# First queries and keys loaded behind the last weights, and one way of making the power of two for all 16 pieces

## The chip, the cores and the metric

The kernel runs on one core of a Trainium2 chip. The core has a matrix engine (PE, TensorE), a vector engine (DVE), a scalar engine (ACT), a general engine (POOL, GpSimd) and a queue engine (SP) that here issues all the transfers. The engines run their own instruction streams in order and wait for one another through semaphores. The metric is the device time of one execution in microseconds; the reported number is the median of several executions.

## The reference

Top-k attention feeds a two-layer perceptron. Cut to what matters, the functions put in a row:

```python
batch, n_heads, seq, head_dim = (8, 8, 576, 64)
top_k = 32
scores = scale * np.matmul(q, k.transpose(0, 1, 3, 2))
kth = np.partition(scores, -top_k, axis=-1)[..., -top_k:-top_k + 1]
mask = scores >= kth
scores = np.where(mask, scores, -1000000000.0)
scores = scores - np.max(scores, axis=-1, keepdims=True)
attn = np.exp(scores)
attn = attn / (np.sum(attn, axis=-1, keepdims=True) + 1e-09)
attn_out = np.matmul(attn, v).astype(np.float32)
...
x = np.ascontiguousarray(attn_out.transpose(0, 2, 1, 3)).reshape(B * S, H * D)
h = x @ w_in
g = np.maximum(0.01 * h, h)
return (g @ w_out).astype(np.float32)
```

x has 4608 rows of 512 numbers, w_in is 512 x 2048 and w_out 2048 x 512.

q, k and v are float32. The two weight matrices come out of `randn(...) * (1.0 / np.sqrt(...))` and are float64, so the kernel has to round 16 MB of 64-bit numbers to float32 before it can use them.

## The kernel before

**The opening: 16 pieces of weights.** The weights lie in DRAM as 16 pieces of 128 x 1024 float64 numbers, 1024 KB each (pieces 0 to 7 are w_in, 8 to 15 are w_out). A double is read as four 16-bit words. `load_weights` (L107 issues the transfer) brings a piece into one of three buffers called raw. `round_weights` is a generator with three parts, and the loop over n at the end of the kernel runs part one of piece n, part two of piece n-1 and part three of piece n-2 in each turn:

- part one: POOL copies the highest word of each number into a tile called top (L124, two buffers); ACT turns the middle words into the destination tile (L125) and the low words into a bf16 tile (L127).
- part two: DVE takes the exponent out of top into the tile scale (L129). For pieces 0 to 13 ACT then makes the power of two from it with the exponential function (L132). For pieces 14 and 15 two DVE instructions make it instead, a clamp and a shift of the exponent into a bf16's place (L135, L136). DVE also takes the mantissa bits (L137) and the sign (L138) out of top; PE adds the three parts of the mantissa in PSUM with six matmuls against scaled identities (L148 to L150).
- part three: DVE joins sign and power of two (L152) and multiplies the sum in PSUM by it into the destination tile (L155; two instructions for pieces 13 and 15, whose sums lie in two tiles).

A transfer into a raw buffer waits until POOL and ACT have read the piece three before. POOL's copy of piece n waits until DVE's L152 of piece n-2 has read the top tile it overwrites.

**Queries and keys.** The 64 heads are taken as 32 pairs. `load_qk(pi)` issues two transfers of 288 KB on SP (L168 for q, L169 for k). In the kernel before, the pairs 0 to 3 are loaded in the turns n = 6 to 9 of the weight loop, each directly behind `load_weights(n + 3)`, so that they stand on SP's queue between the pieces 9 and 13. Everything on SP's queue is issued in the order in which it is written.

**The first scores.** `first_scores(u)` computes the scores of one block of 128 queries: eight short matmuls on PE (L236), then two copies from PSUM on ACT (L241). It is called for the first block in turn n = 13 and for the second in turn n = 16. In the order of ACT's stream, the copies of the first block stand between the exponential of piece 12 and the first activation of piece 14; on PE, its matmuls stand between the sums of piece 12 and those of piece 13.

**The main part.** 144 units follow, one step each. In a step DVE finds the 32 largest scores per row (`top_k`: L250, L255, L258), POOL masks the rest (L268, L269), ACT exponentiates (L272) and normalizes (L284), the result is transposed by DMA through DRAM (L293, L294, L298) or on PE in haste (L308, L314), PE weighs the values (L335), and chunks of finished tokens go through the perceptron on PE (L391 for the first layer, L403 for the second; L359 and L375 for the first two chunks). The order of all this is written out by hand; PE gets portions of perceptron work in fixed slots of each step.

Of the kernel before, what the change touches and what calls it, by code (L numbers as in the profile page):

```python
# [12 lines left out]
BF16 = mybir.dt.bfloat16  # L13
AF = mybir.ActivationFunctionType
ALU = mybir.AluOpType
# [5 lines left out]
def kernel(  # L21
# [13 lines left out]
    nc = tc.nc  # L35
# [9 lines left out]
    HP = DMODEL // P  # L45
# [30 lines left out]
    LN2 = math.log(2.0)  # L76
    least = const.tile([P, 1], F32, name="least")
# [8 lines left out]
    NPIECE = 2 * HP * DFF // WCH  # L86
# [3 lines left out]
    def piece(n):  # L90

        if n < NPIECE // 2:
            j, c = divmod(n, HP)
            return w_in[c][:, j * WCH:(j + 1) * WCH]
        f = 2 * (n - NPIECE // 2)
        return w_out[f // 4][:, f % 4:f % 4 + 2, :].rearrange("p g n -> p (g n)")
# [12 lines left out]
    def round_weights(n):  # L109

        raw = raw_of.pop(n)
        dst = piece(n)
        mid = raw[:, :, 2]
        low = raw.rearrange("p n w -> p (n w)").bitcast(U32).rearrange("p (n w) -> p n w", w=2)[:, :, 0]
        top = raws.tile([P, WCH], U16, name="top", bufs=2)
        scale = raws.tile([P, WCH], U16, name="scale", bufs=2)  # L120
        parts = work.tile([P, 2 * NKC - 1, P], F32, name="wT", bufs=3)
        parts = parts.rearrange("p c n -> p (c n)").bitcast(U16)
        m_top, m_low = parts[:, 0:WCH], parts[:, WCH:2 * WCH].bitcast(BF16)
        nc.gpsimd.tensor_copy(top, raw[:, :, 3])  # L124
        nc.scalar.activation(dst, mid, AF.Copy, bias=-7.0 - 2.0 ** -16, scale=2.0 ** -20)  # L125

        nc.scalar.activation(m_low, low, AF.Copy, bias=128.0, scale=2.0 ** -29)  # L127
        yield
        nc.vector.tensor_scalar(scale, top, 4, 0x7FF, ALU.logical_shift_right, ALU.bitwise_and)  # L129
        if n < NPIECE - 2:  # L130

            nc.scalar.activation(scale.bitcast(BF16), scale, AF.Exp, bias=least, scale=LN2)  # L132
        else:

            nc.vector.tensor_scalar(scale, scale, 1151.0, 896.0, ALU.min, ALU.max)  # L135
            nc.vector.tensor_scalar(scale, scale, 896.0, 128.0, ALU.subtract, ALU.mult)  # L136
        nc.vector.tensor_scalar(m_top, top, 0xF, 0x3F80, ALU.bitwise_and, ALU.bitwise_or)  # L137
        nc.vector.tensor_scalar(top, top, 0x8000, None, ALU.bitwise_and)  # L138
        if n < NPIECE - 4 or n % 2 == 0:
            tag, bufs = ("wide", 2) if n < NPIECE - 4 else ("narrow", 1)  # L140
            pw = ps_sc.tile([P, 2, 512], F32, name=tag, bufs=bufs)
            sums = [(pw[:, h, :], h * 512) for h in range(2)]
            ends = [(pw.rearrange("p h n -> p (h n)"), 0)]
        else:
            ends = sums = [(ps_ml.tile([P, 512], F32, name="pw", tag="ml"), h * 512) for h in range(2)]
        for pw, c in sums:
            at = slice(c, c + 512)
            nc.tensor.matmul(pw, ident_top, m_top[:, at].bitcast(BF16), start=True, stop=False)  # L148
            nc.tensor.matmul(pw, ident, dst[:, at], start=False, stop=False)
            nc.tensor.matmul(pw, ident_low, m_low[:, at], start=False, stop=True)  # L150
        yield
        nc.vector.tensor_tensor(scale, scale, top, ALU.bitwise_or)  # L152
        for pw, c in ends:
            at = slice(c, c + pw.shape[-1])
            nc.vector.tensor_tensor(dst[:, at], pw, scale[:, at].bitcast(BF16), ALU.mult)  # L155
# [5 lines left out]
    def load_qk(pi):  # L161
        if pi % (LOADED + 3) < LOADED:
            qt = loads.tile([P, S], F32, name="qt")
            kt = loads.tile([P, S], F32, name="kt")
        else:
            raw = raws.tile([P, WCH, 4], U16, name="raw").rearrange("p n w -> p (n w)").bitcast(F32)
            qt, kt = raw[:, 0:S], raw[:, S:2 * S]
        nc.sync.dma_start(qt, qT[pi])  # L168
        nc.sync.dma_start(kt, kT[pi])  # L169
        qk_of[pi] = qt, kt  # L170
# [314 lines left out]
    with tc.manual_schedule():  # L485
        last = {p: n for n, u in enumerate(steps) for p in u.pairs}

        def load_more(s):

            for of, load, n, lag in ((v_of, load_v, LOADED_V, LAG + 1), (qk_of, load_qk, LOADED + 3, 8)):  # L490
                while len(of) < NPAIR and (len(of) < n or last[len(of) - n] + lag <= s):
                    load(len(of))
                    if lag > LAG + 1 and len(of) > n:
                        break


        for n in range(3):
            load_weights(n)
        rounding = {}
        for n in range(NPIECE + 2):  # L500
            for i in (n, n - 1, n - 2) if AS_WORDS else ():
                if 0 <= i < NPIECE:
                    if i == n:
                        rounding[i] = round_weights(i)
                    next(rounding[i], None)
            load_weights(n + 3)
            if 6 <= n < 6 + HP:
                load_qk(n - 6)
            elif n == NPIECE - 3:
                first_scores(steps[0])  # L510
            elif n == NPIECE:
                first_scores(steps[1])
            if n == NPIECE - 1:
                load_v(0)
                load_v(1)

        def weights_of(u):
            reciprocals(u)
            normalize(u, 0)
            normalize(u, 1)  # L520

        def values(*place):
            due = [u for n, u in enumerate(steps) if values_at(n) == place]
            if due:
                po = ps_sc.tile([P, 2, 512], F32, name="wide", bufs=2)[:, 0, 0:2 * P]
                po = po.rearrange("p (u n) -> p u n", u=2)
            else:
                return ()
            for n, u in enumerate(due):
                weigh_values(u, po[:, n, :])  # L530
            return [(u, po[:, n, :]) for n, u in enumerate(due)]

        def keep(weighed, *place):
            for u, po in weighed:
                keep_values(u, po)
            attended(*place)

        for s in range(len(steps) + LAG + 1):
            cur, old, older, new = unit(s), unit(s - 1), unit(s - 2), ()
            if s % 2 == 0:  # L540
                new = [u for u in steps[s + 2:s + 4] if u]
            picks = top_k(cur) if cur else iter(())
            budget = slot_budget(s)

            def slot():
                next(picks, None)

            at_first = s < HURRY and s - 2 in HURRIED
            if at_first:
                weights_of(older)  # L550
            slot()
            if old:
                mask(old, 0)
                mask(old, 1)
            late = s < HURRY and not {s - 1, s - 2} & set(HURRIED)
            if older and not late and not at_first:
                weights_of(older)
            mlp_steps(budget)
            weighed = values(s, MIDDLE)
            at_once = s - 2 in HURRIED or any(at == (s, MIDDLE) for at, _ in ready_at)  # L560
            if at_once:
                keep(weighed, s, MIDDLE)
            slot()
            if older and late:
                weights_of(older)
            if s - 2 in HASTY:
                transpose_in_haste(older)
            mlp_steps(budget)
            if old:
                exponents(old, 0)  # L570
            mlp_steps(budget)
            if older:
                keep_transposed(older) if s - 2 in HASTY else transpose(older, lambda: mlp_steps(budget))
            if not older or s - 2 in HASTY:
                mlp_steps(budget)
            slot()
            slot()
            mlp_steps(budget)
            if old:
                exponents(old, 1)  # L580
                sums(old)
            mlp_steps(budget)
            if not at_once:
                keep(weighed, s, MIDDLE)
            if new and s < HURRY:
                scores(new)
            keep(values(s, END), s, END)
            if new and s >= HURRY:
                scores(new)
            budget = slot_budget(s + 1)  # L590
            mlp_steps(budget)
            load_more(s)
        mlp_steps(1e9)
# [58 lines left out]
```

## Time and profile before

| what | value | from |
|---|---|---|
| median of four executions | 1471.62 us | the times |
| lowest, highest | 1469.85, 1472.03 us | the times |
| the profiled execution's own time | 1469.85 us | the times |
| its span, first to last instruction | 1468.0 us | page, head |
| mean granted PE clock over the span | 0.980 | view of the cores |
| PE, DVE, ACT, POOL busy | 1394.6, 1321.5, 1098.1, 1096.2 us | page, part 1 |
| weight loop: from the first transfer's issue to the first `top_k` | 0.72 to 64.69 us | timelines of SP and DVE |
| DVE idle ahead of `rz` (L281), waiting for ACT | 45.0 us in 45 places, the longest 7.7 us | waits of DVE, from 64 us on |
| PE idle from 130 to 240 us | 4.5 us in five places | waits of PE |

What the engines do in stretches of the opening, in us of busy time:

| stretch | PE | DVE | ACT | POOL | GB/s moved |
|---|---|---|---|---|---|
| 10 to 20 | 9.99 | 7.76 | 10.00 | 2.77 | 338 |
| 20 to 30 | 8.44 | 9.27 | 10.00 | 3.63 | 337 |
| 30 to 40 | 8.09 | 8.87 | 9.30 | 3.21 | 407 |
| 40 to 50 | 8.50 | 9.27 | 7.90 | 3.62 | 414 |
| 50 to 60 | 7.30 | 8.70 | 8.56 | 2.63 | 392 |
| 60 to 70 | 8.21 | 9.76 | 3.54 | 0.24 | 110 |

A timeline row gives start and duration in us, the engine, the line, the operation, what it writes and reads, and in brackets the idle time ahead of it with what ended it. Instructions of one engine overlap a little, so a row's duration can be longer than the distance to the next start; sums are made from the starts.

### The profile page before, as it was taken

The numbers are of one execution on the slowest core, as the hardware profiler recorded it, in microseconds if no ns is written. First come the engines' busy times: TensorE is split into PE (matmuls) and PEld (weight loads), VectorE is DVE, ScalarE is ACT, GpSimd is POOL, SyncE is SP. The second block draws the span as 40 slices with busy tenths as digits, with TensorE's granted clock in tenths as the row PEclk, the third lists the DMA queues.
The fourth block names the chain that finished last, engine by engine and source line by source line (L and its number), as shares of the span: only waits on it lengthen the run. The fifth ranks groups of instructions, "written<-read, shape, count | busy, mean of one in ns | idle before, by whom it ended". The sixth has DMA issues, their size and how long they took to land.

```text
span 1468.0 us, 24094 instructions
## 1 busy us (share of the span) xinstructions
PE 1394.6 (95%) x8066; PEld 927.7 (63%) x8068; DVE 1321.5 (90%) x3400; ACT 1098.1 (75%) x1979; POOL 1096.2 (75%) x743
## 2 busy tenths in 40 slices
PE   7717999999999999999999999999999999999999
PEld 2304548575767676767676767666666666666674
DVE  6999999999999999999999999999999999999600
ACT  8657888777887777777777777777777777777710
POOL 3288888888788888787888887878787878787700
PEclk9957999999999999999999999999999999999999
DMA  9724443655366455664566555765457545664510
GB/s 345 287 75 134 138 120 100 187 148 141 96 194 189 137 137 155 171 185 137 146 166 185 151 137 124 195 179 150 126 161 208 137 138 138 162 140 134 148 45 14
DMA packets 388795, 222.29 MB, mean 151 GB/s; under 512 B 333888, under 2 KB 333888, under 8 KB 386624
## 3 DMA queue, kind: packets, MB, share of 16 engines
q1 hardware_dynamic: 388672, 220.77, 53.3%
q8 instruction: 63, 1.03, 0.3%
q14 instruction: 60, 0.49, 0.1%
HBM read 46.14 MB, written 92.01 MB: 94 GB/s over the span
## 4 chain that ended last, share of the span: by engine, by line
PE 80%; DVE 15%; DMA 2%; ACT 1%; issue 1%; POOL 0%; DVEq 0%; ACTq 0%; SPq 0%
PE ph L391 31%; PE pz L403 31%; PE wide L335 10%; DVE tops L255 6%; PE wide L220 6%; DVE pairs L258 5%; PE narrow L220 3%; DVE pairs L250 2%; DMA raw<-in_weights_dram 1%; DMA wT<-apart 1%; DVE w_in L155 1%; DVE scale L152 1%; DVE w_out L155 0%; DVE scale L129 0%; DVE top L138 0%
## 5 line engine op out<-in xcount | busy, mean ns | idle before, releaser
L268 POOL TENSOR_SCALAR pen<-s_sb,tops 128x576 f32<-128x576 f32 x288 | 637.5, 2213 | 208.2 <-DVE tops L255 140.1
L255 DVE MAX8 tops<-pairs 128x8 f32<-128x288 f32 (+1 forms) x1152 | 635.8, 591 | 0.0
L403 PE MATMUL pz<-w_out,gT 128*128 128x512 f32 x1152 | 504.7, 594 | 2.4 <-ACT scale L364 2.4
L391 PE MATMUL ph<-x,w_in 128*128 128x256 f32 x2176 | 482.9, 381 | 0.0
L258 DVE MATCH_REPLACE8 pairs<-tops,pairs 128x288 f32<-128x288 f32 (+1 forms) x864 | 460.0, 537 | 0.0
L391 PEld LDWEIGHTS ph<-x,w_in 128*128 128x128 f32 x2176 | 409.4, 190 | 76.7 <-issue 22.2
L269 POOL TENSOR_TENSOR s_sb<-s_sb,pen 128x576 f32<-128x576 f32 x288 | 406.5, 1411 | 24.1
L403 PEld LDWEIGHTS pz<-w_out,gT 128*128 128x128 f32 x1152 | 216.4, 190 | 267.2 <-issue 262.8
L293 ACT COPY split<-s_sb 128x1152 uint16<-128x1152 uint16 x280 | 309.4, 1146 | 0.0
L284 ACT ACTIVATE s_sb<-s_sb,rz 128x576 f32<-128x576 f32 x288 | 207.6, 773 | 46.8 <-DVE rz L281 46.8
L272 ACT ACTIVATE s_sb<-s_sb,nbias 128x576 f32<-128x576 f32 x288 | 222.3, 772 | 13.8 <-POOL s_sb L269 13.8
L250 DVE TENSOR_TENSOR pairs<-s_sb 128x576 f32<-128x576 f32 x288 | 213.3, 779 | 9.9
L335 PEld LDWEIGHTS wide<-wT,vt 128*64 128x64 f32 x3200 | 161.7, 139 | 66.8 <-issue 34.5
L335 PE MATMUL wide<-wT,vt 128*64 128x128 f32 (+1 forms) x3200 | 179.4, 268 | 24.0 <-ACT s_sb L227 21.1
L227 ACT COPY s_sb<-wide 128x704 f32<-128x704 f32 x142 | 107.1, 755 | 21.1 <-PE wide L220 21.0
L397 ACT ACTIVATE gT<-ph 128x512 f32<-128x512 f32 x136 | 80.6, 592 | 54.2 <-PE ph L391 53.5
L349 ACT COPY x<-wide 128x128 f32<-128x128 f32 (+1 forms) x160 | 32.2, 260 | 111.6 <-PE wide L335 111.4
L220 PE MATMUL wide<-kt,qt 64*128 64x352 f32 (+1 forms) x392 | 75.8, 496 | 26.4 <-ACT s_sb L227 23.6
L412 ACT COPY o_sb<-pz 128x512 f32<-128x512 f32 x36 | 21.0, 585 | 97.3 <-PE pz L403 95.1
L227 ACT COPY s_sb<-narrow 128x448 f32<-128x448 f32 x142 | 68.7, 536 | 0.7
L281 DVE RECIPROCAL rz<-ze 128x2 f32<-128x2 f32 x144 | 22.2, 154 | 45.1 <-ACT ze L277 45.0
L258 DVE MATCH_VALUE_LOAD pairs<-tops,pairs 128x8 f32 x864 | 62.5, 72 | 0.0
(63 smaller groups left out, 621.6 us busy)
## 6 DMA issues: line engine op xcount, KB each, us to landing
apart<-split SPq DMA_DIRECT2D x280, 288.0 KB, 2.1
raw<-in_weights_dram SPq DMA_DIRECT2D x16, 1024.0 KB, 6.7
vt<-in_vk_dram SPq DMA_DIRECT2D x32, 320.0 KB, 3.4
out_dram<-o_sb SPq DMA_DIRECT2D x36, 256.0 KB, 2.6
qt<-in_qT_dram SPq DMA_DIRECT2D x20, 288.0 KB, 3.2
kt<-in_kT_dram SPq DMA_DIRECT2D x20, 288.0 KB, 3.7
raw<-in_qT_dram SPq DMA_DIRECT2D x12, 288.0 KB, 3.6
raw<-in_kT_dram SPq DMA_DIRECT2D x12, 288.0 KB, 3.7
```

Of the source, the lines that this page charges most:

```text
L220: nc.tensor.matmul(to[r0:r0 + u.rows, i, :], qt[d, u.q0:u.q0 + u.rows], kt[d, k0:k1], start=True, stop=True)
L250: nc.vector.tensor_tensor(pairs[:, :, n, :], u.both[:, :, 0:HS], u.both[:, :, HS:S], op)
L255: nc.vector.max(out=u.tops[:, i, r, :], in_=rest[i])
L258: nc.vector.match_replace(out=rest[i], in_to_replace=u.tops[:, i, r, :], in_values=rest[i], imm_value=LOWEST)
L268: nc.gpsimd.tensor_scalar(pen, u.s[i], u.tops[:, i, ROUNDS - 1, 7:8], MASKED, ALU.is_lt, ALU.mult)
L269: nc.gpsimd.tensor_tensor(u.s[i], u.s[i], pen, ALU.add)
L272: nc.scalar.activation(u.s[i], u.s[i], AF.Exp, bias=u.nbias[:, i:i + 1], scale=SCALE, accum_out=u.z[:, i:i + 1])
L284: nc.scalar.activation(u.s[i], u.s[i], AF.Copy, bias=0.0, scale=u.rz[:, i:i + 1])
L293: nc.scalar.copy(split, pairs[:, :, h])
L335: nc.tensor.matmul(po[side * D:(side + 1) * D, o, :], vt[:, c, side, :], u.wT[:, c + side * NKC if c + 1 < NKC else c, r:r + n], start=(c ...
L391: nc.tensor.matmul(ph[:, i, 0:n], w_in[c][:, f * P:(f + 1) * P], x[c][:, 0:n], start=(c == 0), stop=(c == HP - 1),)
L403: nc.tensor.matmul(pz[0:m, 0:DMODEL], gT[:, f, r0:r0 + m], w_out[f // 4][:, f % 4, :], start=(f == 0), stop=(f == NFC - 1),)
```

## The change

All 16 pieces take the exponential on ACT; the two DVE instructions for pieces 14 and 15 are gone. The four pairs of q and k are issued in the turns n = 12 to 15, the first of them behind the last weight transfer. The first block's scores are computed one turn later, n = 14 instead of 13.

```diff
@@ round_weights
         nc.vector.tensor_scalar(scale, top, 4, 0x7FF, ALU.logical_shift_right, ALU.bitwise_and)
-        if n < NPIECE - 2:
-
-            nc.scalar.activation(scale.bitcast(BF16), scale, AF.Exp, bias=least, scale=LN2)
-        else:
-
-            nc.vector.tensor_scalar(scale, scale, 1151.0, 896.0, ALU.min, ALU.max)
-            nc.vector.tensor_scalar(scale, scale, 896.0, 128.0, ALU.subtract, ALU.mult)
+
+        nc.scalar.activation(scale.bitcast(BF16), scale, AF.Exp, bias=least, scale=LN2)
         nc.vector.tensor_scalar(m_top, top, 0xF, 0x3F80, ALU.bitwise_and, ALU.bitwise_or)
@@ the weight loop
             load_weights(n + 3)
-            if 6 <= n < 6 + HP:
-                load_qk(n - 6)
-            elif n == NPIECE - 3:
+
+            if NPIECE - HP <= n < NPIECE:
+                load_qk(n - NPIECE + HP)
+            if n == NPIECE - 2:
                 first_scores(steps[0])
             elif n == NPIECE:
                 first_scores(steps[1])
```

The order of instructions that comes of it: SP issues 16 weight transfers in a row, then the eight of q and k, then the values as before. PE does the first block's eight matmuls between the sums of pieces 13 and 14 (before: 12 and 13). ACT's stream at the end of the loop becomes

```
before: ... L132 of 12 | L241 x2 (first block) | L125, L127 of 14 | L132 of 13 | L125, L127 of 15 | L241 x2 (second block)
after:  ... L132 of 12 | L125, L127 of 14 | L132 of 13 | L241 x2 (first block) | L125, L127 of 15 | L132 of 14 | L132 of 15 | L241 x2 (second block)
```

(the lines named as in the kernel before). Behind that, every engine's instructions are the same and in the same order.

## The prediction

> **What bounds the kernel now.** I read the page's chain of waits first, then the chain in order of time where it changes engine, then the timelines of DVE, ACT and PE around the end of the weight loop.
>
> ```profile
> span 1468.0 us, 24094 instructions
> PE 80%; DVE 15%; DMA 2%; ACT 1%; issue 1%; POOL 0%; DVEq 0%; ACTq 0%; SPq 0%
> ```
>
> ```profile
> 208.53 0.85 DVE pairs L258 x2
> 209.38 0.08 DVE rz L281
> 209.47 0.02 issue
> 209.49 0.79 ACT s_sb L284
> 210.27 0.04 issue
> 210.32 0.66 PE wide L308 x4
> ```
>
> The chain is on DVE until 209.5 us and on PE from there to the end, where PE is busy 1252.0 of 1255 us. So a microsecond that DVE gains before 209 us starts PE's long stretch a microsecond sooner, and nothing behind it is touched by the change. PE itself starts that stretch behind DVE: its sums from 128 us on wait for ACT copies that DVE paces. From 64.69 to 209 us DVE is busy without a wait the profile charges to another engine. What matters is thus the start of the first `top_k` (L250), at 64.69 us.
>
> DVE's rows ahead of it, pieces 13 to 15 of the weights:
>
> ```profile
> 50.89 0.42 DVE L137 TENSOR_SCALAR wT<-top 128x1024 uint16<-128x1024 uint16 x1
> 51.34 0.43 DVE L138 TENSOR_SCALAR top<-top 128x1024 uint16<-128x1024 uint16 x1
> 52.34 0.69 DVE L152 TENSOR_TENSOR scale<-scale,top 128x1024 uint16<-128x1024 uint16 x1 [0.57 <-ACT scale L132]
> ...
> 58.71 0.43 DVE L129 TENSOR_SCALAR scale<-top 128x1024 uint16<-128x1024 uint16 x1
> 59.17 0.43 DVE L135 TENSOR_SCALAR scale<-scale 128x1024 uint16<-128x1024 uint16 x1
> 59.63 0.43 DVE L136 TENSOR_SCALAR scale<-scale 128x1024 uint16<-128x1024 uint16 x1
> 59.97 0.42 DVE L137 TENSOR_SCALAR wT<-top 128x1024 uint16<-128x1024 uint16 x1
> ...
> 64.69 1.42 DVE L250 TENSOR_TENSOR pairs<-s_sb 128x576 f32<-128x576 f32 x2
> ```
>
> One wait, 0.57 us for an exponential, and otherwise DVE runs straight through: it sets the pace, 3.26 us a piece (47.29 to 50.55 from one L129 to the next). ACT's and PE's rows in the same stretch:
>
> ```profile
> 49.06 1.18 ACT L125 ACTIVATE w_out<-raw 128x1024 f32<-128x1024 uint16 x1 [0.67 <-DMA raw<-in_weights_dram]
> ...
> 52.19 1.17 ACT L241 COPY s_sb<-wide 128x576 f32<-128x576 f32 x2
> 53.24 1.18 ACT L125 ACTIVATE w_out<-raw 128x1024 f32<-128x1024 uint16 x1
> 54.31 1.12 ACT L127 ACTIVATE wT<-raw 128x1024 bf16<-128x1024 uint32 x1
> 55.34 1.14 ACT L132 ACTIVATE scale<-scale,least 128x1024 bf16<-128x1024 uint16 x1
> ```
>
> ```profile
> 50.77 1.24 PE L236 MATMUL wide<-kt,qt 64*128 64x288 f32 x8
> ```
>
> ACT was late with piece 12's exponential because piece 13 came late from DMA (0.67 us here, and 0.33, 0.77 and 0.66 us at pieces 10 to 12). The first block's copies did not wait.
>
> **The change, part by part.**
>
> *Weights sooner.* In the trace's DMA records the q and k of one pair hold the queue for 1.5 us (each 288 KB about 0.75 us), four times ahead of later weights. Without them piece 13 lands sooner than its 49.04. ACT, unhindered, takes a piece in 3.13 us (17.49 to 20.62); from piece 8's L125 at 30.54 that puts piece 13's L125 at 46.2 and piece 12's exponential at 48.3, done 49.5. Even if the weights keep the slow pace of pieces 3 to 8 (one per 3.1 us), piece 13 lands at about 45.6. DVE wants that exponential at 51.68 (L138 at 51.34 plus 0.34, the distance from L138 to L152 elsewhere). So the wait goes: 52.34 - 51.68 = 0.66 us. Nothing more is gained sooner: DVE sets the pace, POOL's copies follow its L152, and weight transfers are issued behind POOL's copies.
>
> *Four DVE instructions removed.* L129 to L137 takes 55.73 - 54.46 = 1.27 us with the pair and 0.34 without (50.89 - 50.55), so 0.93 us for each of two pieces, 1.86 us, all on DVE's path. Alone, these two parts would put L250 at 64.69 - 0.66 - 1.86 = 62.17.
>
> *The new wait.* Piece 14's exponential is now ACT's, and in ACT's stream it stands behind the first block's copies (L241) and L125 and L127 of piece 15. The copies wait for PE's L236, and that now stands behind piece 13's sums, which start after DVE's L137 at 51.31. Step by step: six matmuls, 2.6 us (48.10 to 50.69 for piece 12), so PE is free at 53.94; L236 takes 1.24, done 55.18; copies from 55.21, 1.05 us to the next start (52.19 to 53.24); L125 at 56.26; L127 at 57.33; exponential of piece 14 at 58.36, done 59.50. DVE would want it at 58.27 (62.17 less the 3.92 from L152 of piece 14 to L250, 60.77 to 64.69) and gets it at 59.54: 1.27 us lost. Behind the waiting L152 stand the last products and every `top_k`. Next late would be piece 15's exponential, 59.39 to 60.53 on ACT; DVE wants it at 59.54 + 0.79 + 1.14 = 61.47, so it is covered by 0.9 us. Piece 14's sums, delayed behind L236 to 55.2 to 57.8, are wanted at 60.33; piece 15's need its L127, done 58.45, and end at 60.6, wanted at 62.25. The second block's copies move to about 62 and are wanted a whole step (8.8 us) later.
>
> *q and k later.* The first pair is issued behind the last weight: POOL is done with piece 12 at 47.05 as before, so SP issues the weight at 47.1 and q, k by 48.3. Early bound for the landing: 1.0 us to the first packet (piece 0: 0.72 to 1.74), 2.5 us for the weight (pace of pieces 0 to 2), 1.5 for the pair, 0.4 to be signalled: 52.4. Late bound: weights at 3.1 us each from piece 8 (28.57 on the median DMA engine), held by the issue to about 51.5, the slowest engine 1.9 us behind as at piece 8 (30.52), plus 1.5: 54.9. PE wants it at 53.94: cost 0 to 1.0 us. I take 0, since between 31 and 47 us the queue now has gaps in which the slow engine catches up. The other pairs are wanted by the second block at 60.6 and by the next scores (L220) at about 63.6; at 1.5 us a pair they are there by 58. The values move little and are first wanted at 110.66.
>
> *Not shown.* Before L129 at 37.52 DVE stood 0.45 us for which no wait is shown, just as ACT waited for a weight. If it came from the queue's crowding it goes too: 0 to 0.45 us more gained; I take 0.
>
> Sum: 0.66 + 1.86 - 1.27 = **1.25 us sooner**; L250 at 63.45. The profiled execution took 1469.85 us (1.85 around its span) and would take 1468.6; its time is the lowest of the four, 1.77 under the median, so the median goes from 1471.62 to **1470.4**.
>
> [...]
>
> **Rivals.**
>
> *A, the wait at piece 14 does not bite.* For it: ACT has 52.6 to 55.2 us idle in my account, so any slip of mine in the order frees a lot. Against: ACT's and PE's streams are in order and as written. Gain 0.66 + 1.86 = 2.52, with the 0.45 at most 2.97: 1469.1 to 1468.65.
>
> *B, slower: q and k land too late for the first block.* For it: k took a median of 8.1 us from issue to landing in the opening, which from 47.9 is 56.0. Against: it then stood behind two weights and other pairs. PE's L236 would slip from 53.94 to 56.0, and copies, L125, L127, exponential, L152 with it: 2.06 - 1.25 = 0.8 us slower, 1472.4. It decides from a landing at 53.94 + 1.25 = 55.2 on.
>
> *C, the gain does not reach the end*: PE's own work from 128 us on sets the end whatever DVE does. For: PE waits only 4.5 us in all between 130 and 240. Against: these waits are behind DVE, and PE's start at 128.39 is too. 1471.6.
>
> **How the numbers follow.** Forecast 0.53 (gain 0.25 to 1.7, so 1469.9 to 1471.4), A 0.15, B 0.12, C 0.08; 0.12 for what I have not seen. The four runs spread over 2.2 us, so a median may be off by some 0.5. The range, from A's end less that to B's plus that: 1468.2 to 1472.8. About 0.2% is what a measurement of this kernel can tell from no change, here 2.9 us: faster is under 1468.7, slower over 1474.6. Faster: 0.07 of A and 0.06 of the unseen, 0.13; slower: 0.02 of B's tail and 0.05 of the unseen, 0.07; within, 0.80.
>
> **What would show it.** L250 at 63.4 to 63.5 with no wait at piece 12's L152 and about 1.3 us at piece 14's, for ACT; ACT idle 2.6 us ahead of the first L241, for PE; no DMA wait on ACT from piece 10 on; the handover from DVE to PE near 208 us. I am wrong if L250 moves and the end does not follow, if L236 waits for a DMA, or if the piece-14 wait is missing.

## The result, and the profile after

| | kernel before | changed kernel |
|---|---|---|
| median | 1471.58 us (54 runs, 1469.39 to 1475.24) | 1469.01 us (34 runs, 1467.83 to 1472.66) |
| ratio to before, with its 95% interval | | 0.9985 (0.998 to 0.999) |
| profiled execution: its own time, its span | 1469.85, 1468.0 us | 1468.56, 1466.5 us |
| first `top_k` starts | 64.69 us | 63.55 us |
| handover from DVE to PE (first L308 / L303 on PE) | 210.32 us | 209.33 us |

By the ratio the changed kernel is faster by 0.15%, which is 2.2 us, and the interval reaches from 1.5 to 2.9 us; the two medians as they stand differ by 2.6 us. The forecast was 1.2 us. In the changed kernel the lines behind the exponential stand five earlier and the exponential one: it is L131, mantissa and sign bits are L132 and L133, the joining L147, the product L150, the first block's matmuls and copies L231 and L236, `top_k` begins with L245, the hasty transposes are L303.

The head and the chain of waits of the changed kernel's page, and its chain in order of time at the handover (start, duration, what):

```profile
span 1466.5 us, 24092 instructions
PE 85%; DVE 10%; ACT 2%; DMA 2%; issue 1%; SPq 0%; POOL 0%; DVEq 0%; ACTq 0%
```

```profile
207.54 0.85 DVE pairs L253 x2
208.39 0.09 DVE rz L276
...
208.50 0.78 ACT s_sb L279
...
209.33 0.66 PE wide L303 x4
```

The handover runs over the same instructions as before, 1.0 us sooner. The chain's shares moved from DVE to PE in two other places. From 121 to 157 us it now runs over ACT and PE, mostly PE, where it stayed on DVE before; and behind 300 us it no longer turns off to DVE, on which it spent 50 us there before. From 157 us to the handover it is on DVE again.

DVE's timeline of the changed kernel around pieces 12 to 15:

```profile
51.31 0.43 DVE L133 TENSOR_SCALAR top<-top 128x1024 uint16<-128x1024 uint16 x1
51.65 0.68 DVE L147 TENSOR_TENSOR scale<-scale,top 128x1024 uint16<-128x1024 uint16 x1
...
57.89 0.43 DVE L133 TENSOR_SCALAR top<-top 128x1024 uint16<-128x1024 uint16 x1
59.62 0.69 DVE L147 TENSOR_TENSOR scale<-scale,top 128x1024 uint16<-128x1024 uint16 x1 [1.30 <-ACT scale L131]
...
63.55 1.42 DVE L245 TENSOR_TENSOR pairs<-s_sb 128x576 f32<-128x576 f32 x2
```

L147 of piece 12 follows L133 at 0.34 us, so the wait for a late weight is gone; L147 of piece 14 waits 1.30 us for ACT. ACT's timeline shows why:

```profile
51.41 1.14 ACT L131 ACTIVATE scale<-scale,least 128x1024 bf16<-128x1024 uint16 x1
55.27 1.18 ACT L236 COPY s_sb<-wide 128x576 f32<-128x576 f32 x2 [2.73 <-PE wide L231]
56.34 1.17 ACT L125 ACTIVATE w_out<-raw 128x1024 f32<-128x1024 uint16 x1
57.40 1.15 ACT L127 ACTIVATE wT<-raw 128x1024 bf16<-128x1024 uint32 x1
58.43 2.19 ACT L131 ACTIVATE scale<-scale,least 128x1024 bf16<-128x1024 uint16 x2
```

ACT stands idle for 2.73 us ahead of the first block's copies, and the exponential of piece 14 is queued behind them. No wait of ACT for a weight is left from piece 10 on.

### The profile page after: what moved, and what is told of

The parts are those of the page before. It is cut to its first block, busy times and chain, and to the rows that moved or that the text cites. A ratio compares the mean times of both kernels' runs of the same rounds, so it can differ in the third digit from the quotient of the medians.

```text
span 1466.5 us, 24092 instructions
## 1 busy us (share of the span) xinstructions
PE 1392.7 (95%) x8066; PEld 927.1 (63%) x8068; DVE 1319.8 (90%) x3396; ACT 1099.7 (75%) x1981; POOL 1096.2 (75%) x743
## 3 DMA queue, kind: packets, MB, share of 16 engines
q8 instruction: 63, 1.03, 0.3%
## 4 chain that ended last, share of the span: by engine, by line
PE 85%; DVE 10%; ACT 2%; DMA 2%; issue 1%; SPq 0%; POOL 0%; DVEq 0%; ACTq 0%
PE ph L386 32%; PE pz L398 31%; PE wide L330 11%; PE wide L215 6%; DVE tops L250 3%; PE narrow L215 3%; DVE pairs L253 3%; PE ph L354 1%; DVE pairs L245 1%; ACT split L288 1%; DVE w_in L150 1%; DMA wT<-apart 1%; DMA apart<-split 1%; DVE scale L147 1%; ACT s_sb L222 1%
## 5 line engine op out<-in xcount | busy, mean ns | idle before, releaser
L245 DVE TENSOR_TENSOR pairs<-s_sb 128x576 f32<-128x576 f32 x288 | 213.4, 779 | 10.3 <-ACT s_sb L279 0.5
```

Source lines behind the costliest of these rows:

```text
L245: nc.vector.tensor_tensor(pairs[:, :, n, :], u.both[:, :, 0:HS], u.both[:, :, HS:S], op)
```

## The experiments

Three theories were tried. Theory 1 is the prediction's account with the sizes of the first profile. Theory 2 says that the wait for late weights in the kernel before differs from run to run and that its first profile caught a small one. Theory 3 came up with the first experiments: part of every kernel's spread is PE's clock.

The readings that the experiments share, in us, from the timelines of DVE and PE:

| profile | piece 9's L129 to the first `top_k` | first `top_k` | from there to the handover |
|---|---|---|---|
| before, first | 27.17 | 64.69 | 145.63 |
| b1, b2, b3: before again | 28.88, 28.37, 27.33 | 65.47, 65.64, 64.46 | 145.63, 146.01, 147.10 |
| changed, first | 26.06 | 63.55 | 145.78 |
| e0, a2, a3: changed again | 26.05, 26.07, 26.74 | 63.42, 63.50, 64.12 | 147.11, 145.94, 147.11 |
| e1: q and k moved alone | 26.53 | 63.88 | 147.11 |
| e2: exponential alone | 26.92 | 64.42 | 145.84 |
| e3, e6: copies last | 24.68, 24.68 | 61.46, 62.11 | 145.79, 147.12 |
| e5: copies last, PE's wait filled | 24.68 | 61.47 | 145.61 |
| e4: two DVE instructions for all pieces | 31.30 | 76.45 | 147.11 |

### e0: the changed kernel once more

> The changed kernel once more, unaltered. Theory 1 (the account of the prediction: only the start of the first top_k moves the end, and it moved by 1.1 us in the profiles) expects 1.1 to 1.3 us under the kernel before. Theory 2 (in the kernel before, the weights behind q and k are late by an amount that differs from run to run, and its profiled run was a lucky one; the changed kernel has slack there) expects 2.0 to 2.6 us under it. Both expect the first top_k at 63.4 to 63.7 us.

Median 1469.9 us against 1471.55 beside it, ratio 0.9989 (0.998 to 0.9997), 1.6 us faster. That lies between the two theories, and the interval, 0.4 to 2.9 us, holds both. The first `top_k` came at 63.42 us, as expected. But the handover came at 210.53, 1.2 us later than in the first profile though DVE was 0.13 sooner. That gave theory 3; its rows are in the last section.

### e1: q, k and the first scores moved, the DVE instructions kept

```diff
-        nc.scalar.activation(scale.bitcast(BF16), scale, AF.Exp, bias=least, scale=LN2)
+        if n < NPIECE - 2:
+            nc.scalar.activation(scale.bitcast(BF16), scale, AF.Exp, bias=least, scale=LN2)
+        else:
+            nc.vector.tensor_scalar(scale, scale, 1151.0, 896.0, ALU.min, ALU.max)
+            nc.vector.tensor_scalar(scale, scale, 896.0, 128.0, ALU.subtract, ALU.mult)
```

> q and k moved behind the last weights, first scores a turn later, but the two DVE instructions for pieces 14 and 15 kept. Both theories expect the first top_k at 64.0 us (64.69 less 0.66) and no wait of ACT for weights. Theory 1: 0.6 to 0.7 us under the kernel before, which can hardly be told from it. Theory 2: 1.4 to 2.0 us under it, since the typical lateness of the weights, more than the 0.66 us of the profiled run, goes as a whole.

Median 1469.72 us against 1471.55, ratio 0.9988 (0.9979 to 0.9996): 1.8 us faster, first `top_k` at 63.88. Theory 2's size (1.4 to 2.0), though the interval, 0.6 to 3.1 us, reaches to theory 1's. One of its readings missed: ACT did wait for a weight once more, 0.29 us, and it cost nothing. PE's row of the first scores (L235 here) shows something else:

```profile
56.15 1.24 PE L235 MATMUL wide<-kt,qt 64*128 64x288 f32 x8 [2.20 <-DMA kt<-in_kT_dram]
```

The first pair's k landed at 56.01 us, later than the late bound of 54.9 in the prediction, and PE waited 2.20 us for it. In e1 that cost DVE nothing, since no exponential stands behind the copies on ACT. In the changed kernel two do.

### e2: the exponential in all pieces, everything else as before

```diff
-        if n < NPIECE - 2:
-            nc.scalar.activation(scale.bitcast(BF16), scale, AF.Exp, bias=least, scale=LN2)
-        else:
-            nc.vector.tensor_scalar(scale, scale, 1151.0, 896.0, ALU.min, ALU.max)
-            nc.vector.tensor_scalar(scale, scale, 896.0, 128.0, ALU.subtract, ALU.mult)
+        nc.scalar.activation(scale.bitcast(BF16), scale, AF.Exp, bias=least, scale=LN2)
```

> The exponential in all 16 pieces, q and k and the first scores where they were. Worked out from the rows of the kernel before: DVE is spared 1.86 us, waits about 0.92 us for piece 13's exponential, which ACT ends at 56.48, and the first top_k starts at 63.8 us, 0.9 us sooner. Theory 1: 0.9 us under the kernel before. Theory 2: 0.5 to 0.9 us under it, the late weights stay; so under theory 2 this part is clearly smaller than the other, under theory 1 larger.

Median 1470.93 us against 1471.55, ratio 0.9993 (0.9984 to 1.0001): 0.6 us, not to be told from none. The first `top_k` was expected at 63.8 and came at 64.42, because the weights were later than in the first profile. DVE's rows of e2 (here L129 is the first of part two, L146 the joining, L130 the exponential):

```profile
50.97 0.43 DVE L129 TENSOR_SCALAR scale<-top 128x1024 uint16<-128x1024 uint16 x1 [0.54 <-POOL top L124]
52.98 0.69 DVE L146 TENSOR_TENSOR scale<-scale,top 128x1024 uint16<-128x1024 uint16 x1 [0.79 <-ACT scale L130]
57.16 0.69 DVE L146 TENSOR_TENSOR scale<-scale,top 128x1024 uint16<-128x1024 uint16 x1 [0.83 <-ACT scale L130]
```

The third row is the wait for piece 13's exponential, worked out as 0.92 and measured as 0.83. The first two are the late weights, which this kernel keeps: 1.33 us here where the first profile of the kernel before had 0.57. By the medians the move of q and k brings more (1.8 us) than the instructions taken off DVE (0.6 us), as theory 2 has it. But the two intervals, 0.6 to 3.1 and -0.1 to 2.4 us, overlap widely, so that it is the larger part is not shown.

### b1, b2, b3: the kernel before, three more profiles

> The kernel before, unaltered, for another profile. Theory 1 expects the first top_k at 64.69 us as in the first profile, give or take 0.2. Theory 2 expects it later in most profiles, by up to 2 us and on the average about 0.8, with ACT waiting longer for the weights of pieces 9 to 13. Theory 3 (the runs differ because the clock of PE drops to half for one window of 3.41 us when PE's wait of 2.14 us near 195 us falls inside one window) expects the handover from DVE to PE 145.7 us behind the first top_k where the clock stays up, and 147.1 us behind it where it drops.

> As b1: a further profile of the kernel before. Theory 1: first top_k at 64.69 us; theory 2: later in most profiles, by 0.8 us on the average; theory 3: handover 145.7 or 147.1 us behind it, by the clock.

> As b1 and b2: a further profile of the kernel before. Theory 1: first top_k at 64.69 us; theory 2: later in most profiles, by 0.8 us on the average; theory 3: handover 145.7 or 147.1 us behind it, by the clock.

The first `top_k` came at 65.47, 65.64 and 64.46 us. DVE's waits in b1, from its timeline:

```profile
44.65 0.69 DVE L152 TENSOR_TENSOR scale<-scale,top 128x1024 uint16<-128x1024 uint16 x1 [0.32 <-ACT scale L132]
48.63 0.69 DVE L152 TENSOR_TENSOR scale<-scale,top 128x1024 uint16<-128x1024 uint16 x1 [0.63 <-ACT scale L132]
51.12 0.43 DVE L129 TENSOR_SCALAR scale<-top 128x1024 uint16<-128x1024 uint16 x1 [0.47 <-POOL top L124]
53.12 0.69 DVE L152 TENSOR_TENSOR scale<-scale,top 128x1024 uint16<-128x1024 uint16 x1 [0.77 <-ACT scale L132]
```

Four waits where the first profile had the last alone, and all behind ACT's waits for weights (0.65, 0.74, 0.75 and 1.28 us at pieces 10 to 13). From piece 9's L129 to the first `top_k` the four profiles of the kernel before took 27.17 to 28.88 us, 27.94 on the average. The first profile was the shortest of the four, as theory 2 has it; two of the other three were longer by over a microsecond and b3 by 0.16. DVE's waits between 40 and 58 us add up to 0.57 us in the first profile and to 2.19, 1.58 and 0.72 us in b1, b2 and b3, which accounts for these differences. By the start of `top_k` itself, which the expectation names, b3 is a miss: at 64.46 us it came sooner than in the first profile, since its piece 9 began 0.39 us sooner. Theory 3's reading held: PE's clock dropped in b3 alone, and its handover is the one at 147.10.

### a2, a3: the changed kernel, two more profiles

> The changed kernel unaltered, for another profile. The first two have the first top_k at 63.55 and 63.42 us. Theory 2 expects 63.3 to 63.7 us again, with no wait of DVE between 40 and 58 us, where the four profiles of the kernel before lie between 64.46 and 65.64. If it too is spread over a microsecond, the spread is not that of the late weights.

> As a2: the changed kernel unaltered, for a further profile. Theory 2: first top_k at 63.3 to 63.7 us and no wait of DVE between 40 and 58 us.

No wait of DVE between 40 and 58 us in either, though ACT waited for one weight in each (0.50 and 0.95 us). a2 is as the first two; in a3 the first `top_k` came at 64.12, outside what was expected, and for another reason. PE's row of the first scores in a3:

```profile
54.61 1.24 PE L231 MATMUL wide<-kt,qt 64*128 64x288 f32 x8 [0.65 <-DMA kt<-in_kT_dram]
```

Here the last part of k landed at 54.48 us, and PE waited 0.65 us for it. DVE's wait at piece 14 grew to 1.97 us. That is the mechanism of rival B, in one of the four profiles of the changed kernel and within the bounds that the prediction gave (52.4 to 54.9; the others landed at 53.20 to 53.76). Those four flatter the bounds. Eight profiles have q and k in this place of the queue, the four and e1, e3, e5 and e6: the first k landed at 52.62 to 53.76 us in five of them, at 54.48 here, at 55.31 in e3 and at 56.01 in e1.

### e3 and e6: the first block's copies behind all exponentials

```diff
     def first_scores(u):
...
+        u.first = ps
+
+    def keep_first_scores(u):
         u.both = work.tile([P, 2, S], F32, name="s_sb", bufs=5)
...
-            if n == NPIECE - 2:
+            if n == NPIECE - 1:
                 first_scores(steps[0])
             elif n == NPIECE:
+                keep_first_scores(steps[0])
                 first_scores(steps[1])
+                keep_first_scores(steps[1])
```

> The changed kernel, with the first block's matmuls behind piece 14's sums and their copies behind piece 15's exponential on ACT, so that no exponential stands behind a copy. Both theories: no wait of DVE at piece 14, first top_k at 62.1 to 62.4 us, 1.2 to 1.4 us sooner than in the changed kernel, and the end with it. Theory 1: 2.5 us under the kernel before; theory 2: 3.2 to 3.8 us under it. If the wait at piece 14 did not cost the end anything, the time is that of the changed kernel.

> The kernel of e3 unaltered, beside e5 on the same chip. Theory 2, with the first measurement: 3.2 to 4.1 us under the kernel before, first top_k at 61.4 to 62.2 us. Theory 1: 2.5 us under it.

e3: 1467.48 us against 1471.55, ratio 0.997 (0.9959 to 0.9981). e6: 1469.44 us against 1473.04, ratio 0.9975 (0.9965 to 0.9984). So 4.4 and 3.7 us faster than the kernel before (e3's interval, 2.8 to 6.0 us, leaves out the 2.5 of theory 1; e6's, 2.4 to 5.2, just holds it), and faster than the changed kernel by 2.4 us in the first set (1469.9 against 1467.48; no interval was taken for this pair). The first `top_k` of e3, expected at 62.1 to 62.4 us, came at 61.46, because its piece 9 began 0.7 us sooner than in the changed kernel's first profile; e6's, at 62.11, is as expected. The exponentials of e3 on ACT, and its DVE at the end of the opening:

```profile
54.91 1.15 ACT L127 ACTIVATE wT<-raw 128x1024 bf16<-128x1024 uint32 x1
55.97 2.17 ACT L131 ACTIVATE scale<-scale,least 128x1024 bf16<-128x1024 uint16 x2
58.05 1.14 ACT L239 COPY s_sb<-wide 128x576 f32<-128x576 f32 x2
```

```profile
57.19 0.43 DVE L133 TENSOR_SCALAR top<-top 128x1024 uint16<-128x1024 uint16 x1
57.54 0.68 DVE L147 TENSOR_TENSOR scale<-scale,top 128x1024 uint16<-128x1024 uint16 x1
...
61.46 1.42 DVE L248 TENSOR_TENSOR pairs<-s_sb 128x576 f32<-128x576 f32 x2
```

Both exponentials run without a gap ahead of the copies, L147 of piece 14 follows L133 at 0.35 us, and from piece 9 to the first `top_k` it is 24.68 us in all three profiles of this order, 1.38 less than the 26.06 of the changed kernel: about the wait of 1.30 us at piece 14. A weight that was late here (ACT waited 0.41 us for piece 15) cost nothing. Nor did the late k: it landed at 55.31 us, and PE's first scores, now behind piece 14's sums, start at 56.58 without a wait for it. Whether this cover is why the timed gain over the changed kernel is larger than 1.38 us is not shown.

### e4: the two DVE instructions for all pieces

```diff
-        if n < NPIECE - 2:
+        if n < 0:
```

> The kernel before with the power of two made by the two DVE instructions in all 16 pieces, the exponential gone from ACT. If DVE sets the pace of the opening and a microsecond of it is a microsecond at the end, 14 more pairs of instructions cost 14 x 0.93 = 13.0 us, less the 0.57 us of waiting for the exponential: first top_k at about 77.1 us, time about 1484. The rival that ACT or the transfers set the pace expects much less, down to no loss, as ACT is spared 14 x 1.03 us. The rival that PE's own work sets the end expects the first top_k later and the end not.

First `top_k` at 76.45 us, time 1483.75 us (two runs) against 1471.45 beside it, ratio 1.0082 (1.0052 to 1.0111, that is 7.7 to 16.3 us). 12.3 us at the end for 11.8 at the first `top_k` (11.4 against the mean of the four profiles of the kernel before, 65.07). So DVE sets the pace of the opening, and, as far as this interval can tell, a microsecond there is a microsecond at the end; the rivals that put the end to ACT, the transfers or PE's own work fall. The first `top_k` came 0.7 us sooner than expected. From piece 9 on the sum is right: 31.30 us, 4.13 more than in the first profile of the kernel before, for five pairs at 0.93 less the wait of 0.57. The shortfall lies ahead of piece 9, where the kernel before had waits of its own (1.26 us for POOL at 9.35 us, which e4 does not have). A row of ACT in e4 shows what cover looks like:

```profile
42.36 1.17 ACT L125 ACTIVATE w_out<-raw 128x1024 f32<-128x1024 uint16 x1 [3.60 <-DMA raw<-in_weights_dram]
```

ACT waits up to 3.6 us for a weight and DVE never waits for ACT from 14 us on, since ACT has 1.03 us less to do in every piece.

### e5: PE's wait near 193 us filled

```diff
-        for i in range(4):
-            nc.tensor.transpose(pt[:, i, :], g_of[j][:, i * P:(i + 1) * P], ident)
+        for i in range(4 * times):
+            nc.tensor.transpose(pt[:, i % 4, :], g_of[j][:, i % 4 * P:(i % 4 + 1) * P], ident)
```

`times` is 4 in the one place of the kernel of e3 behind which PE waits 2.14 us, else 1.

> The kernel of e3 with 12 more transposes on PE, written over the same result, in the wait of 2.14 us that lies near 193 us here. They take 12 x 0.11 = 1.3 us of that wait and nothing waits for them. Theory 3 (part of the spread of every kernel is PE's clock dropping for one window behind this wait): no drop of the clock near 195 us, handover always 145.7 to 146.0 us behind the first top_k, median 0 to 1.3 us under that of e3 by the share of runs in which it dropped, and fewer runs above the lowest by over 1 us. If the wait is not the cause, the clock still drops in some profile and the median is that of e3 or up to 1.3 us more.

The clock did not drop and the handover came 145.61 us behind the first `top_k`, and the 11 runs lie closer together (1469.38 to 1471.15; e6 beside it 1467.28 to 1471.72). One profile without a drop says little by itself, since seven of the other 13 have none either. And the median is 1470.23 us, 0.8 above e6, where 0 to 1.3 below was expected; the ratio is 0.9983 (0.9974 to 0.9991) to the kernel before, an interval that overlaps e6's. In the profile the loss lies late: from the handover to PE's last matmul the profile took 1257.75 us, where the other 13 took 1253.6 to 1256.4, with PE waiting for values (1.7 us) and for transposed weights (2.1 us in six places). Whether the twelve transposes are the cause of these late transfers was not tried and stays open; as an improvement the edit failed.

## Why the prediction was right, point by point

The direction, the mechanism and the range held (1468.2 to 1472.8 with a median of 1469.01). The size was too small: 1.2 us forecast, 2.2 measured with an interval from 1.5. Two sums have small slips that change nothing: 62.17 less 3.92 is 58.25, so the new wait comes to 1.29 us, and 1472.4 plus 0.5 is 1472.9.

- *DVE's start of `top_k` sets the end.* Held: e4 moved the one by 11.8 and the other by 12.3 us. The handover moved with it in every profile, at 145.6 to 146.0 us, or 147.1 where PE's clock dropped. One reading was off: the chain is not on PE alone from there to the end, since behind 300 us the chain of that profile spends 50 us on DVE and 15 us on DMA. PE's time from the handover to its last matmul is not fixed either, 1253.6 to 1256.4 us in the 13 profiles without e5; PE waits there for transposed tiles from DMA, 1.8 us in the first profile and 3.5 us in a2. The prediction had no term for this. It adds to the spread but not to the gain: the mean is 1254.6 us for the four profiles of the kernel before and for the four of the changed one.
- *Weights sooner, "52.34 - 51.68 = 0.66 us".* As far as four profiles can show, this is the term that was mis-sized. In the profile it was built on it was exact (L147 of piece 12 at 51.65), but that execution's weights were the least late of four. Over four profiles the stretch from piece 9 to `top_k` is 27.94 us before, so the term is 0.66 + 27.94 - 27.17 = 1.43 us on the average. From four profiles that lie up to 1.7 us apart this average is good to some 0.4 us (estimate). The changed kernel does not share that spread; in its place it has a smaller one, the 0.65 us of a3.
- *Four DVE instructions removed, 1.86 us, and the new wait, 1.27 us.* Both held: 0.34 us again from L129 to the mantissa bits, and a wait of 1.30 us in three of four profiles. ACT's idle time ahead of the copies was put at 2.6 and was 2.73. In e3, where the wait is gone, the stretch to `top_k` is 1.38 us shorter; the timed gain over the changed kernel, 2.4 us, is in the same direction and larger.
- *q and k later, cost 0 to 1.0, taken as 0.* In the changed kernel's own profiles, landings at 53.20 to 53.76 in three cost nothing and 54.48 in the fourth cost 0.65: 0.16 on the average. The reason given, that the slow engine catches up in the gaps, does not always hold: of the eight profiles with this order of transfers k was in time for 53.94 in five and not in a3, e3 and e1, and the late bound of 54.9 was passed in two. That the four profiles of the changed kernel got off so lightly is in part luck: a landing at 56.01, as in e1, would cost it about 2.1 us (estimate: less the 53.94 at which PE wants it).
- *The wait of 0.45 us not shown, ahead of piece 9's L129.* The timeline has it as 0.51 us behind DVE's own L155. It stayed, 0.51 to 0.53 us, in each of the other 13 profiles, with q and k moved or not: at the same instruction in 12 of them, and in e4, where DVE has more instructions per piece, at piece 7's L129 (36.74 us). So q and k in the queue are not its cause; what is was not found.
- *The median, "1.77 under the median".* The difference between the profiled execution and the median was carried over as a constant. It is not one: by the four profiles part of it was the late weights, which the change takes away, and so the median fell by more than the profile (2.2 against 1.3 us).

With the measured sizes the sum is 1.43 + 1.86 - 1.30 - 0.16 = 1.8 us. The table gives 1.71 (27.94 less 26.23, the means of four), which is no test, since the 1.43 is taken from it; the two timed comparisons, 1.6 and 2.2 us, are one. The rivals: A did not occur in the changed kernel, but e3 built it, and from piece 9 to `top_k` it is 2.49 us shorter than the first profile of the kernel before (27.17 less 24.68), where A said 2.52; C fell with e4; B occurred in part, in one of four profiles of the changed kernel, and in e1 k landed when B said, at 56.0.

## What to carry to other kernels

A wait for DMA in one profile is one draw: DVE's waits from 40 to 58 us, behind late weights, came to 0.57, 2.19, 1.58 and 0.72 us in four profiles of the kernel before. Where a change removes such a wait, its size should come from several profiles, since the median holds the average of what is removed and not the one drawn. Where an in-order engine is given work that it must do after a wait, the place in its stream decides: here two copies that DVE first read 8 us after they began stood ahead of two exponentials, for the first of which DVE waited 1.30 us, and setting them last took another 1.5 us off the stretch to `top_k` (26.23 less 24.68, the means), after 1.7 us for the change itself.

## What the runs showed of the hardware

**In 6 of 14 profiles PE's granted clock fell behind a wait of 2.14 us, in e0 to 0.50 for 3.40 us.** PE waits 2.13 to 2.15 us for the same value of ACT in every profile but e5's (ending between 193 and 197.4 us; in e4, whose opening is longer, at 207.8). In e0 the clock dropped behind it, in the first profile of the changed kernel it stayed. PE's timeline in e0, then in the changed kernel's first profile:

```profile
194.81 2.92 PE L398 MATMUL pz<-w_out,gT 128*128 128x512 f32 x4 [2.14 <-ACT scale L359]
```

```profile
195.07 1.98 PE L398 MATMUL pz<-w_out,gT 128*128 128x512 f32 x4 [2.14 <-ACT scale L359]
```

And e0's busy time in three stretches (length, PE, weight loads, DVE, ACT, POOL, then granted clock, DMA share and GB/s):

```profile
192.30:195.70 3.40, 1.26 (x6) 0.61 (x5) 3.40 (x8) 3.40 (x6) 2.20 (x4) 1.00 0.59 133
195.70:199.10 3.40, 3.40 (x15) 1.10 (x17) 3.37 (x9) 2.60 (x6) 3.32 (x2) 0.50 0.48 178
199.10:202.50 3.40, 3.40 (x32) 1.41 (x28) 3.40 (x12) 3.23 (x6) 3.22 (x3) 1.00 0.66 123
```

The same matmuls take 2.92 instead of 1.98 us, and the handover is 1.3 us later. It happened in 6 of 14 profiles, of the kernel before and of changed ones alike: there these four matmuls take 2.62 to 3.66 us, in the eight others 1.98. In the first profiles of the two kernels the changes of the clock stand multiples of 3.41 us apart (58.03, 44.37, 3.41, 13.65 and 1334.61 us from one to the next in that of the kernel before). Counted off in steps of 3.41 us from the clock's changes in its own trace, the wait lay within one step in all six, as theory 3 has it, and across the end of one in the seven others that have the wait: 1.29 us of it ahead of that end and 0.84 behind in the first profile of the changed kernel. The closest is b1, where all but 0.17 us of the wait lay within one step, and the clock stayed:

```profile
194.88:198.29 3.41, 1.44 (x4) 0.68 (x4) 3.38 (x8) 3.41 (x7) 2.23 (x3) 1.00 0.46 103
```

PE was busy 1.44 of these 3.41 us, and 1.26 of the 3.40 ahead of e0's drop. That the place of the wait and the drop go together is what these traces show; why they do is not shown.

The granted clock differs in the opening too. In the first profile of the kernel before it rose at 13.39 us (two matmuls of L149 take 1.91 us ahead of that and 1.02 behind it), DVE waited 0.89 us for PE's first sums and piece 9's L129 came at 37.52; in b1 it rose at 10.56, DVE did not wait there, and L129 came at 36.59. So L129 came 0.93 us sooner in b1, but in e2, where the clock rose at 10.85, it came at 37.50, behind a wait of 0.57 us for ACT at 18.52.

**In a3 and e1 one of the 16 parts of k's transfer landed 1.26 and 2.09 us behind the others.** The traces signal each of these transfers in 16 parts. In a3 half of k's parts had landed by 53.12 us, 15 by 53.22 and the last at 54.48; in e1 15 had landed by 53.92 and the last at 56.01; in e0 half had landed by 53.09 and the last at 53.20. Which run gets the lag was not found.
